# A larger planned margin on the q, k and v weight loads of a fused attention and feed-forward kernel

## The chip, the cores and the metric

The kernel runs on one core of one Trainium2 chip. The metric is the device time of one execution in microseconds, the median over runs. A core has TensorE (PE; its weight loads are PEld), VectorE (DVE), ScalarE (ACT), GpSimd (POOL) and SyncE (SP), which here issues all DMAs; the engines run side by side and meet at semaphores.

## What is computed

```python
def _A_ref(x, wqkv, wo):                      # x: 1 x 2048 x 576, 32 heads of 18
    qkv = (x @ wqkv) ...                      # q, k, v by heads
    scores = einsum("bhqd,bhkd->bhqk", q, k) * 18 ** -0.5
    mask = (i - j >= 0) & (i - j < 256)       # causal window of 256
    p = softmax(where(mask, scores, -1e9))
    return einsum("bhqk,bhkd->bhqd", p, v) ... @ wo

def _B_ref(x, w_gate, w_up, w_down):          # 576 -> 4608 -> 576
    return (sigmoid(x @ w_gate) * (x @ w_up)) @ w_down

xn = layernorm(x)
return x + _A_ref(xn) * silu(_B_ref(xn))
```

All inputs and the output are bf16; x has 2048 tokens of 576 features.

## The kernel before

The 2048 tokens are worked in four stages of 512 tokens, and each stage has four token blocks of 128. A stage normalises its blocks, brings them into `xn` (features on partitions, tokens along the free axis), projects q, k and v, and then runs two things interleaved on TensorE: the gate and up products of the feed-forward, 36 tiles of 128 hidden features, and the windowed attention, in eight head groups of four heads. The down projection (`f2`) closes the stage, and the next stage's projections stand inside it.

The matmuls have only 64 rows of contraction, so they go in pairs: one on the upper and one on the lower half of the array, side by side.

**A program that is planned, not written in order.** `Builder` makes a list of operations, each with an engine, an estimated length, the operations it depends on and a priority. `schedule` (L1083) simulates the five engines with these estimates and places the operations one by one: of those enabled on an engine it takes the one with the smallest start time plus `prio * PRIO_NS` (L1151 to L1164). The order in which operations are placed on an engine is the order in which that engine executes them. The estimates set only this order and the choice of PSUM banks; on the chip the waits are semaphores. For a DMA the planner computes when it should land, and its users are ready at

```python
                elif o.lane is not None:
                    t = o.done + o.slack
```

(L1210), so `slack` is a margin that the planner adds to one DMA's landing. It appears in no instruction.

**The first stage.** SyncE issues the four blocks of x, then twelve loads of `wqkv`: four parts each for q, then v, then k (`QKV_LOAD`), then the gate and up weights in groups of three tiles. `load9` splits a weight into four parts: parts 0 and 1 hold the first features for the lower and the upper half of the array, parts 2 and 3 the rest. `build_weights` sets the margin of the twelve loads:

```python
            for o in self.op_wqkv[j]:
                o.slack = QKV_SLACK
```

For the first stage TensorE transposes the normalised blocks (L487; two transposing steps a block, of 8 and of 10 matmuls), and ScalarE copies each result into `xn` (L499). `project` (L506, matmuls at L513) makes one projection of one block: 9 feature groups, two matmuls each, into one pair of PSUM banks, taken from (4, 5), (6, 7), (0, 1), (2, 3). For q of blocks 0 and 1 (`Q_SPLIT`) it is cut: a first part of 4 feature groups (8 matmuls), which needs only load parts 0 and 1 and the first of the two `xn` copies, and a second part of 5 (10 matmuls), which needs all four. ScalarE and VectorE then evict q and k (L567, into `pk` for block 0 and `expr` for the others) or v (L613, into `vau`). The places in `expr` are cleared by ScalarE first (L380), the third of these clearings after block 3's `xn` copies. When k of a block is evicted, a transposing DMA (L250) brings its q and k into `qkp`. VectorE spreads k from there (`kd`, L660), TensorE makes scores (L676, four steps a head group, units 0 to 3), ScalarE the exponential (L691), VectorE the mask (L705), TensorE the product with v (L733), VectorE the transposes and the division (L749 to L766).

The feed-forward steps (`f`, L884) use PSUM banks 4 to 7; the tanh on ScalarE (L898) and the multiply on VectorE (L902) free them. The scores use banks (0, 1) and (2, 3) in turn; the exponential frees them.

The order of TensorE at the start, before the change (`tr` are transposes; q0 is q of block 0; a and b are the first and second part):

```
warm-up, tr0, tr1, q0a, tr2, q0b, q1a, tr3, q1b, q2, v0, v1, v2, k0, v3, k1, q3, k2, k3, feed-forward
```

Of the kernel before, what the change touches and what calls it, by code (L numbers as in the profile page):

```python
# [100 lines left out]
QKT_BEHIND = {3: 0, 4: 1}  # L101
WARM = 10
X0_SLACK = -250.0
QKV_SLACK = 0.0
X_PRIO = (-9, -9, -9, -9)
QKV_LOAD = (-8, -6, -7)
W_PRIO = (-5, -4, -3, -2)
# [103 lines left out]
class Builder:  # L211
# [191 lines left out]
    def build_weights(self):  # L403
        wq = self.wqkv
        self.op_wqkv = [None] * 3
        for j in range(3):
# [3 lines left out]
            for o in self.op_wqkv[j]:  # L410
                o.slack = QKV_SLACK

# [932 lines left out]
```

## Time and profile before

| | |
|---|---|
| median of 3 runs | 561.78 us |
| lowest, highest | 561.67, 562.17 us |
| the profiled execution's own time | 561.61 us |
| its span | 559.9 us |
| TensorE busy | 552.2 us (99%) |
| VectorE, ScalarE, GpSimd busy | 317.7, 274.7, 30.0 us |
| DMA | 73.22 MB, mean 131 GB/s |

The profile is of one execution. Times are microseconds from the start of the span. "Releaser" is what ended an engine's wait; "idle" is rest of the engine just before an instruction. Matmuls overlap, and their ends are modelled, so the start to start distance tells more than the length of one.

### The profile page before, as it was taken

Reading aid. Unit: us, or ns where it says so; the run is one execution under the profiler, and the core shown is the slowest. Engines: PE = TensorE matmul, PEld = TensorE weight load, DVE = VectorE, ACT = ScalarE, POOL = GpSimd, SP = SyncE. Lnnn points to the kernel's source line nnn. Section 1 sums busy time; section 2 is a strip of 40 time slices with the busy share of each in tenths; the row PEclk is TensorE's granted clock in tenths of the full one; section 3 lists DMA queues with packets and bytes.
Section 4 is the critical chain, followed back from the end, with each engine's and each line's share of the span. In section 5 each row is a group of like instructions: output and inputs, shape, how many; then the busy total and the mean of one; then the engine's idle time right before and its main releaser. Section 6 shows DMA issues by size and latency. Waiting matters only on the chain.

```text
span 559.9 us, 16728 instructions
## 1 busy us (share of the span) xinstructions
PE 552.2 (99%) x7115; PEld 310.3 (55%) x7138; DVE 317.7 (57%) x911; ACT 274.7 (49%) x394; POOL 30.0 (5%) x58
## 2 busy tenths in 40 slices
PE   8999999999999999999999999999999999999997
PEld 5755555458555555455755555545665555554554
DVE  6436999334157989522417899841331788575012
ACT  8436876114076778221408776622131887482021
POOL 3000110100000100100000011010000000001000
PEclk9999999999999999999999999999999999999999
DMA  8999779859945665441993556543399354751010
GB/s 202 222 207 232 171 189 212 233 92 135 184 103 129 133 155 130 105 77 36 157 217 75 130 126 150 118 99 64 59 170 194 76 129 108 170 131 42 1 43 21
DMA packets 125921, 73.22 MB, mean 131 GB/s; under 512 B 54680, under 2 KB 125336, under 8 KB 125848
## 3 DMA queue, kind: packets, MB, share of 16 engines
q1 hardware_dynamic: 125848, 72.16, 61.3%
q8 instruction: 56, 0.92, 0.7%
q14 instruction: 17, 0.14, 0.1%
HBM read 55.48 MB, written 2.36 MB: 103 GB/s over the span
## 4 chain that ended last, share of the span: by engine, by line
PE 97%; DMA 1%; SPq 1%; issue 0%; ACT 0%; DVE 0%; ACTq 0%
PE ps L884 50%; PE ps L1009 23%; PE ps L513 9%; PE ps L676 6%; PE ps L733 4%; PE ps L802 3%; PE ps L1040 2%; DMA wqkv_sb<-in_A_wqkv_dram 1%; SPq L251 1%; DMA qkp<-pk 1%; ACT pk L567 0%; DVE expr L1073 0%; ACT expr L1071 0%; PE ps L487 0%; DVE expr L1075 0%
## 5 line engine op out<-in xcount | busy, mean ns | idle before, releaser
L884 PE MATMUL ps<-xn,wgs 64*128 64x512 bf16 x2522 | 299.7, 376 | 0.0
L884 PEld LDWEIGHTS ps<-xn,wgs 64*128 64x128 bf16 x2522 | 121.8, 94 | 113.6 <-issue 1.4
L691 ACT ACTIVATE expr<-ps 128x1024 bf16<-128x1024 f32 (+1 forms) x152 | 149.6, 1031 | 20.5 <-PE ps L676 20.5
L902 DVE SCALAR_TENSOR_TENSOR hT<-tring,ps 128x512 bf16<-128x512 bf16 x144 | 98.3, 683 | 63.3 <-PE ps L884 36.4
L1009 PE MATMUL ps<-wd_sb,hT 128*128 128x64 bf16 (+1 forms) x1057 | 131.1, 284 | 2.1 <-issue 1.1
L898 ACT ACTIVATE tring<-ps 128x512 bf16<-128x512 f32 x144 | 87.4, 607 | 91.8 <-PE ps L884 70.4
L1009 PEld LDWEIGHTS ps<-wd_sb,hT 128*128 128x128 bf16 x1080 | 68.2, 98 | 65.5 <-issue 2.5
L1071 ACT ACTIVATE expr<-ps 128x576 bf16<-128x576 f32 (+2 forms) x17 | 10.6, 623 | 127.8 <-PE ps L1009 120.2
L705 DVE TENSOR_TENSOR expr<-expr,m 128x256 bf16<-128x256 bf16 (+1 forms) x272 | 60.0, 265 | 4.3 <-ACT expr L691 4.1
L1073 DVE SCALAR_TENSOR_TENSOR expr<-expr,ps 128x576 bf16<-128x576 bf16 (+2 forms) x17 | 12.2, 719 | 84.1 <-ACT expr L1071 84.1
L676 PE MATMUL ps<-qkp,kd 64*128 64x320 bf16 (+4 forms) x720 | 57.1, 252 | 0.0
L513 PE MATMUL ps<-wqkv_sb,xn 64*128 64x288 bf16 x864 | 54.5, 283 | 0.5 <-DMA wqkv_sb<-in_A_wqkv_dram 0.4
L660 DVE TENSOR_SCALAR kd<-qkp,hm 128x256 bf16<-128x256 bf16 x176 | 40.5, 290 | 22.5 <-DMA qkp<-pk 20.8
L676 PEld LDWEIGHTS ps<-qkp,kd 64*128 64x128 bf16 x720 | 34.1, 94 | 34.1 <-issue 2.2
L513 PEld LDWEIGHTS ps<-wqkv_sb,xn 64*128 64x128 bf16 x864 | 44.4, 94 | 9.4 <-issue 1.4
L749 DVE STREAM_TRANSPOSE pk<-ps 128x512 f32<-128x512 f32 x32 | 21.5, 700 | 15.8 <-PE ps L733 15.8
L715 POOL COPY qkp<-qkp 128x256 bf16<-128x256 bf16 x24 | 10.8, 450 | 271.3 <-DVE kd L660 271.3
L766 DVE STREAM_TRANSPOSE op__63<-pk 128x512 bf16<-128x512 bf16 x32 | 22.2, 700 | 0.0
L733 PEld LDWEIGHTS ps<-expr,vau 64*32 64x32 bf16 x1440 | 18.1, 92 | 7.4 <-issue 4.7
L733 PE MATMUL ps<-expr,vau 64*32 64x320 bf16 (+4 forms) x1440 | 20.8, 254 | 0.0
L802 PE MATMUL ps<-wo_sb,oT 64*128 64x288 bf16 x288 | 18.7, 283 | 0.1
L613 DVE CAST vau<-ps 64x288 bf16<-64x288 f32 x32 | 14.6, 457 | 7.2 <-PE ps L513 6.6
(52 smaller groups left out, 192.5 us busy)
## 6 DMA issues: line engine op xcount, KB each, us to landing
wgs<-in_B_w_gate_dram SPq DMA_DIRECT2D x47, 240.0 KB, 3.8
wgs<-in_B_w_up_dram SPq DMA_DIRECT2D x47, 240.0 KB, 4.8
wgs<-in_B_w_up_dram SPq DMA_DIRECT2D x47, 192.0 KB, 4.0
wgs<-in_B_w_gate_dram SPq DMA_DIRECT2D x47, 192.0 KB, 4.6
wd_sb<-in_B_w_down_dram SPq DMA_DIRECT2D x9, 576.0 KB, 7.4
xf<-in_A_x_dram SPq DMA_DIRECT2D x18, 144.0 KB, 2.4
out_dram<-xf SPq DMA_DIRECT2D x15, 144.0 KB, 2.0
xr<-in_A_x_dram SPq DMA_DIRECT2D x14, 144.0 KB, 4.5
```

Source lines behind the costliest of these rows:

```text
L513: r = e.matmul(self.bank(ps, HV, hf), self.xn[r0:r0 + 64, k, i * P:(i + 1) * P], self.wqkv_sb[r0:r0 + 64, j, k, :], start=(k == 0), stop=( ...
L660: return e.tensor_scalar(dst, src, self.hm[:, half:half + 1], None, ALU.mult)
L676: i = e.matmul(self.bank(ps, 512, r)[:, pos * 64:(pos + n) * 64], w, self.qkp[r0:r0 + 64, hg, q0 * 64:(q0 + n) * 64], start=True, stop=Tru ...
L691: return e.activation(self.expr[:, es, :, 0:ncol], src, ACTF.Exp, scale=SM_SCALE)
L705: return e.tensor_tensor(ap, ap, m, ALU.mult)
L733: r = e.matmul(self.bank(ps2[s_])[32 * cg:32 * cg + 32, q0 * 64:(q0 + n) * 64], vf[:, v0:v0 + 32], self.expr[p0:p0 + 64, es, cg % 2, pos * ...
L766: t2 = self.op("DVE", dve_ns(CH), lambda e, on=on: e.transpose(self.op_[:, hg % NOT, :], on.rearrange("p g d -> p (g d)")), f"t2:{c}:{hg}" ...
L802: r = e.matmul(self.bank(ps2[w], HV, n), self.oT[r0:r0 + 64, kt, qi * P:(qi + 1) * P], self.wo_sb[r0:r0 + 64, kt, n * HV:(n + 1) * HV], st ...
L884: return e.matmul(self.bank((pg, pu)[gu][ft]), w, self.xn[r0:r0 + 64, i, :], start=first, stop=last, tile_position=(r0, 0))
L898: return e.activation(self.tring[:, st_, :], self.bank(ps), ACTF.Tanh, scale=0.5)
L902: return e.scalar_tensor_tensor(self.hT[:, ft, :], self.tring[:, st_, :], 1.0, self.bank(ps), ALU.add, ALU.mult)
L1009: r = e.matmul(self.ps[:, b + n0:b + n1], lhsT, self.wd_sb[:, q, fl, n0:n1], start=(ft == 0), stop=(ft == NFT - 1))
```

## The change

```diff
@@ -101,7 +101,7 @@
 QKT_BEHIND = {3: 0, 4: 1}
 WARM = 10
 X0_SLACK = -250.0
-QKV_SLACK = 0.0
+QKV_SLACK = 300.0
 X_PRIO = (-9, -9, -9, -9)
 QKV_LOAD = (-8, -6, -7)
 W_PRIO = (-5, -4, -3, -2)
```

The planner takes the twelve loads as landing 300 ns later. The plan that comes out has the same operations; SyncE and GpSimd keep their order. TensorE's order at the start becomes

```
warm-up, tr0, tr1, q0a, tr2, q1a, q0b, tr3, q1b, q2, q3, v0, v1, v2, k0, v3, k1, k2, k3, feed-forward
```

The banks of the later projections follow: q3 takes (6, 7), v0 (0, 1), v1 (2, 3), v2 (4, 5), k0 (6, 7), and so on, where v0 had (6, 7). ScalarE evicts q3 ahead of v0; VectorE does so too, and copies the lower half of the mask (L371) just ahead of the first eviction of q instead of behind it. Further on, around feed-forward tiles 17 to 25 of the first stage, the order shifts by a few places on three engines. On TensorE, the four score steps of head group 3 stand between other numbers of feed-forward matmuls:

```
before: f x10, sc3.0, f x8,  sc3.1, f x14, sc3.2, f x8,  sc3.3, f x10, sc4.0
after:  f x14, sc3.0, f x14, sc3.1, f x4,  sc3.2, f x14, sc3.3, f x4,  sc4.0
```

On ScalarE the tanh of tiles 20 and 21 change places with exponentials of group 3. On VectorE the transposes, divisions, masks and the multiplies of the tiles 17 to 24 are dealt differently among one another. From there on the order of every engine is as before, in this stage and the three others.

## Prediction

> **What bounds the kernel now.** I read the page first: its span, the busy shares, the clock and the chain.
>
> ```profile
> span 559.9 us, 16728 instructions
> PE 552.2 (99%) x7115; PEld 310.3 (55%) x7138; DVE 317.7 (57%) x911; ACT 274.7 (49%) x394; POOL 30.0 (5%) x58
> PEclk9999999999999999999999999999999999999999
> PE 97%; DMA 1%; SPq 1%; issue 0%; ACT 0%; DVE 0%; ACTq 0%
> ```
>
> TensorE works 552.2 of 559.9 us at full granted clock and carries 97% of the chain. A new order of the same matmuls can therefore give at most the 7.7 us in which it rests, and in the stage that is reordered only what it rests there. The view of waits, for TensorE over the whole run, has five rows:
>
> ```profile
> PE ps L388 <- DVE hm L373: 1.5, 1, 1.5
> PE ps L1009 <- issue: 1.1, 7, 0.2
> PE ps L513 <- DMA wqkv_sb<-in_A_wqkv_dram: 0.4, 1, 0.4
> PE ps L1009 <- ACT pk L567: 0.2, 1, 0.2
> PE ps L487 <- DVE xnr L461: 0.2, 1, 0.2
> ```
>
> One row belongs to the projections (L513): a single wait of 0.4 us for their weights. The timeline shows where it stands and what runs around it (start, length, engine, line, operation, count).
>
> ```profile
> 2.67 8.03 SPq L251 DMA_DIRECT2D wqkv_sb<-in_A_wqkv_dram  x12
> 7.04 0.67 PE L513 MATMUL ps<-wqkv_sb,xn 64*128 64x288 bf16 x8
> 8.75 1.28 PE L513 MATMUL ps<-wqkv_sb,xn 64*128 64x288 bf16 x18 [0.39 <-DMA wqkv_sb<-in_A_wqkv_dram]
> 9.64 0.46 DVE L567 CAST pk<-ps 128x288 bf16<-128x288 f32 x1 [0.43 <-PE ps L513]
> 9.85 0.44 PE L487 MATMUL ps<-op__63,xnr 64*128 64x64 bf16 x18
> 10.11 11.96 PE L513 MATMUL ps<-wqkv_sb,xn 64*128 64x288 bf16 x190
> 10.13 0.20 DVE L371 COPY m<-m 64x192 bf16<-64x192 bf16 x1
> 10.18 1.19 ACT L499 ACTIVATE xn<-ps 128x512 bf16<-128x512 bf16 x2
> 11.26 0.42 ACT L567 ACTIVATE expr<-ps 128x288 bf16<-128x288 f32 x1
> 11.55 1.07 ACT L380 ACTIVATE expr<-expr 128x1024 uint32<-128x1024 uint32 x1
> 15.25 0.27 PEld L513 LDWEIGHTS ps<-wqkv_sb,xn 64*128 64x128 bf16 x6 [0.24 <-issue]
> 21.89 17.66 PE L884 MATMUL ps<-xn,wgs 64*128 64x512 bf16 x162
> ```
>
> The 18 matmuls at 8.75 are the second q part of block 0 (10) and then the first q part of block 1 (8). They step in pairs: (9.85 - 8.75) / 9 = 0.122 us a pair, so a first part takes 0.49, a second part 0.61, a whole projection 1.10. The chain of waits names what the second part waits for:
>
> ```profile
> 4.79 3.82 DMA wqkv_sb<-in_A_wqkv_dram
> 8.61 0.14 issue
> ```
>
> The fourth q load, issued at 4.79, lands at 8.61, and TensorE starts 0.14 later. There is a second, smaller wait that the view of waits does not name. From 10.11 to 21.89 are 11.78 us for 190 matmuls; 95 pairs at 0.122 are 11.6, so 0.15 to 0.2 is lost, and the weight loads show one break, at 15.25. There the first k projection stands. The last of the 12 loads (the fourth k load) in the view of the tile, and its time to landing:
>
> ```profile
> L251 SPq DMA_DIRECT2D wqkv_sb<-in_A_wqkv_dram x1: 617/617/617, 10.1 to 10.1; - x1
> DMA to landing us min/median/max: 5.1/5.1/5.1
> ```
>
> It lands at about 15.2, just where the break is: k of block 0 waits for its weights too, about 0.15 us.
>
> **The change part by part.** Nothing is added or taken away: the same matmuls, evictions and DMAs, in the same order on SyncE and GpSimd. Three things move.
>
> First, the first q part of block 1 goes ahead of the second part of block 0. It needs only the first two q loads, which were there when block 0's first part began at 7.04, and the xn copies of block 1, which also free its bank:
>
> ```profile
> 7.50 0.72 ACT L499 ACTIVATE xn<-ps 128x640 bf16<-128x640 bf16 x1
> 8.64 0.70 ACT L499 ACTIVATE xn<-ps 128x640 bf16<-128x640 bf16 x1
> ```
>
> The first of these rows is that copy's second half: it ends at 8.22, and with 0.14 from release to start (the row of 8.61) the part begins at 8.36 and steps until 8.85. By then the load of 8.61 is there, so block 0's second part follows without a wait, 8.85 to 9.46. Block 3's transposes take 10.11 - 9.85 = 0.26; their bank is free when the second row ends at 9.34, plus 0.14 = 9.48 for their second half, which is in time. Block 1's second part starts at 9.72 instead of 10.11: 0.39 gained.
>
> Part of it is given back. q of block 2 writes the bank from which block 0's q is evicted. That eviction now follows a part that began at 8.85 and not 8.75, so it runs from 9.74 to 10.20 (0.46 us on VectorE), and block 2 starts at 10.34, against 9.72 + 0.61 = 10.33 without a wait: 0.01 lost. VectorE's mask copy (0.20, at L371), which now stands ahead of that eviction, fits into the 0.43 us of rest in the row of 9.64 and costs nothing.
>
> Second, q of block 3 comes straight after q of block 2, at 10.34 + 1.10 = 11.44, ahead of all v. It needs block 3's xn. ScalarE makes that after its half of block 0's eviction, which ends at 9.74 + 0.42 = 10.16 (the length of the row of 11.26); two copies take 1.19, so 11.35, plus 0.14 = 11.49. A new wait of 0.05. Taken together the projections now run 0.34 us ahead. The eviction of this q waits for ScalarE's clearing (1.07 us, at L380) and ends near 13.7; the projection that reuses its bank comes at 15.9, so that wait is covered by 2 us. If the clearing stood ahead of the xn copies, 1.07 us would be on the path; the planned order has it behind them.
>
> Third, what moves back: v by one projection and k of block 0 by one. v's loads had caused no wait and get 0.8 us more. k of block 0 starts at 15.28 - 0.34 + 1.10, near 16.0, when its load of 15.2 is there: the second wait, 0.15, goes as well.
>
> The sum: 0.34 + 0.15 = 0.49, say 0.5 us, and the feed-forward starts at 21.4 instead of 21.89. From both sides: the two waits whole give 0.39 + 0.15 = 0.54 and no more can come out of this stage; if the loads land where TensorE is anyway late, nothing is gained; below nothing it goes only by a new wait, which is a rival below.
>
> The planner's clock also moves a little, and near 63 us it deals the third group's score steps anew: between them stand 14, 14, 4, 14 and 4 feed-forward matmuls where 10, 8, 14, 8 and 10 stood. Work is equal; what can differ is the wait of a score step for the exponential that frees its bank.
>
> ```profile
> 64.03 0.38 PE L676 MATMUL ps<-qkp,kd 64*128 64x320 bf16 x4
> 65.33 1.68 PE L884 MATMUL ps<-xn,wgs 64*128 64x512 bf16 x14
> 66.84 0.38 PE L676 MATMUL ps<-qkp,kd 64*128 64x320 bf16 x4
> 69.17 0.38 PE L676 MATMUL ps<-qkp,kd 64*128 64x320 bf16 x4
> 64.30 0.60 ACT L898 ACTIVATE tring<-ps 128x512 bf16<-128x512 f32 x1 [0.33 <-PE ps L884]
> 64.79 1.93 ACT L691 ACTIVATE expr<-ps 128x1024 bf16<-128x1024 f32 x2
> ```
>
> On the old clock the three score steps now fall at 64.46, 66.19 and 66.84. ScalarE: exponential 64.96 to 65.98, tanh to 67.06 (0.6), second exponential to 68.0, third to 68.9 (1.02 each, overlapping by 0.1). The next group's first score step, at 69.17, needs the third: 68.9 + 0.14 = 69.06. It holds, with 0.1 us to spare. VectorE's transposes and masks around 62 to 72 us are dealt differently too, and are off the path while the matmuls' banks come free in time. I cost this move at nothing.
>
> Does the gain live to the end? What follows must not be bound by transfers on fixed times. SyncE issues the same list from 2.67 on and does not move. Rows of the views of tiles: the first group of gate and up weights, its last issue and its landings; the last two transposes of q and k, likewise; and the VectorE step that needs the last of them:
>
> ```profile
> L251 SPq DMA_DIRECT2D wgs<-in_B_w_up_dram x2: 626/1100/1575, 11.4 to 13.7; - x2
> DMA to landing us min/median/max: 5.0/5.5/5.8
> L250 SPq DMA_TRANSPOSE qkp<-expr x2: 2210/2372/2533, 37.5 to 39.8; - x2
> DMA to landing us min/median/max: 4.5/5.4/6.4
> 46.78 0.67 DVE L660 TENSOR_SCALAR kd<-qkp,hm 128x256 bf16<-128x256 bf16 x3
> ```
>
> The first group is there by 13.7 + 5.8 = 19.5 and is needed at 21.4. The last transpose, issued at 39.8, lands by 46.2; the VectorE step on it stands at 46.78 and comes to 46.3, so 0.1 us is left, and the scores behind it come 1 us later still. After that no transfer is named among TensorE's waits, in any stage, and those that SyncE issues behind a wait for TensorE move with it. So everything behind shifts together.
>
> **The sum against the times.** The profiled execution took 561.61 us (span 559.9 and 1.7 around it); the median of the three runs shown is 561.78, 0.17 more. Off the median the 0.5 gives 561.3. No change by a measurement of this kernel is about 0.2%, 1.1 us, so this gain, 0.09%, lies within it.
>
> A rule of the Trainium skill on the loads ("DMA: Bandwidth & Descriptors", Anatomy of one DMA) puts a transfer at about 2.0 us and its bytes at 436 GB/s, fitted on DMAs that GpSimd issues; for 180 KB that would be an estimated 2.4 us, all q weights would be there at 7.2, and the change would gain nothing. The trace disagrees: 3.8 us for that load and 5.1 for the last. What the traces leave of this rule is the second rival, at 0.10.
>
> **The rivals.**
>
> Given back in part (chance 0.14): the next release after the projections is late. For it, q of block 2 and q of block 3 start within 0.05 us of theirs, so 0.1 to 0.3 more on ScalarE goes straight onto the path. Against it, nothing later needs either. Time 561.5.
>
> No gain (0.10): the waits are an accident of the profiled execution, the loads land earlier otherwise, or a fixed transfer such as the transpose near 46 us takes the lead back. The view of the tile has, for all 12 of these loads:
>
> ```profile
> DMA to landing us min/median/max: 3.3/3.9/5.1
> ```
>
> With the quickest, 3.3 us, the fourth q load would be there at 8.1 and the part would wait 0.02. Against it, the profiled execution with both waits is quicker than the median. Time 561.8.
>
> The page's row of the multiply that frees a feed-forward bank:
>
> ```profile
> L902 DVE SCALAR_TENSOR_TENSOR hT<-tring,ps 128x512 bf16<-128x512 bf16 x144 | 98.3, 683 | 63.3 <-PE ps L884 36.4
> ```
>
> Slower (0.10): ScalarE becomes the bound near 69 us. If the third exponential ends after 69.03, the next score step waits, the tanh behind it is late, the VectorE multiply behind that too, and the feed-forward finds no bank: 1.02 + 0.60 + 0.69 = 2.3 us, less 0.5, so 563.6. For it, the margin of 0.1; against it, a late release costs only its own lateness, usually, because 14 matmuls (1.5 us) follow.
>
> Faster by more than 0.2% (0.06): the loads land later without the profiler and both waits are longer. It needs 1.1 us; 560.5.
>
> **How the numbers follow.** The forecast, 561.3, has 0.60. Forecast, part and no gain together, 0.84, lie between 561.2 and 561.8; runs of one kernel differ by 0.5 (561.67 to 562.17), so the range is 560.9 to 562.2. Chances: faster 0.06, same 0.84, slower 0.10.
>
> **What would show it.** Right: no wait on the q weights, or one below 0.1; block 1's first part at 8.4 and its second near 9.7; no break at the first k projection; the feed-forward at 21.4; the span 0.5 shorter, and no rest of TensorE near 64 to 69. Wrong: a wait for ScalarE at L513 above 0.1, a wait at L676 or L884 near 69, or a feed-forward that starts at 21.4 and a second stage that starts as late as before.

## The result and the profile after

| | before | after |
|---|---|---|
| median (22 runs each, side by side) | 561.98 us | 561.23 us |
| lowest, highest | 561.29, 562.82 | 560.85, 561.64 |
| ratio, 95% interval | | 0.9987 [0.9981, 0.9992] |
| the profiled execution | 561.61 us, span 559.9 | 560.9 us, span 559.2 |
| feed-forward starts | 21.89 us | 21.37 us |
| final projection (L1040) starts | 547.80 us | 547.06 us |

The change gains 0.75 us by the medians (0.4 to 1.1 by the interval), 0.73 us by the two profiles. Both lie within the 0.2% that was called no change beforehand. A later series of the changed kernel gives 561.24 beside a median of 561.88 for the kernel before: 0.64. Two executions of the later runs (580.26 us of the kernel before and 580.66 of the last variant below) were slow at a granted clock of 0.95 and are left out of the medians here. Forecast were 561.3 us and a gain of 0.5.

TensorE at the start, in the timeline of the kernel after (start, length, engine, line, operation, count; in brackets the rest before it and what ended it), with the rows of ScalarE that mattered:

```profile
6.88 0.67 PE L513 MATMUL ps<-wqkv_sb,xn 64*128 64x288 bf16 x8
7.86 0.54 PE L487 MATMUL ps<-op__63,xnr 64*128 64x64 bf16 x18 [0.32 <-DVE mv L454]
8.35 1.28 PE L513 MATMUL ps<-wqkv_sb,xn 64*128 64x288 bf16 x18
9.46 0.43 PE L487 MATMUL ps<-op__63,xnr 64*128 64x64 bf16 x18
9.72 11.82 PE L513 MATMUL ps<-wqkv_sb,xn 64*128 64x288 bf16 x190
21.37 2.34 PE L884 MATMUL ps<-xn,wgs 64*128 64x512 bf16 x20
9.73 0.41 ACT L567 ACTIVATE pk<-ps 128x288 bf16<-128x288 f32 x1 [0.35 <-PE ps L513]
10.04 1.19 ACT L499 ACTIVATE xn<-ps 128x512 bf16<-128x512 bf16 x2
```

The 18 matmuls that stood at 8.75 behind a wait of 0.39 now stand at 8.35 with none: the first part of block 1 (8 matmuls), and behind it the second part of block 0 (10). The last 190 begin at 9.72 instead of 10.11, and the start of the feed-forward is 11.65 us behind them, not 11.78: 95 pairs at 0.122 without a break. The stage is 0.52 us shorter.

The view of waits for TensorE, whole run, has two rows in the kernel after:

```profile
PE ps L388 <- DVE hm L373: 1.5, 1, 1.5
PE ps L487 <- DVE mv L454: 0.3, 1, 0.3
```

The row for the weights is gone, but so are the L1009 rows of 1.1 and 0.2 us, which this change cannot have touched. A second profile of the very same kernel has them back. From its page and its view of waits, and behind them the row of the page of the first profile:

```profile
L1009 PE MATMUL ps<-wd_sb,hT 128*128 128x64 bf16 (+1 forms) x1057 | 131.1, 285 | 2.1 <-issue 1.1
PE ps L1009 <- issue: 1.1, 7, 0.2
PE ps L1009 <- ACT pk L567: 0.2, 1, 0.2
```

```profile
L1009 PE MATMUL ps<-wd_sb,hT 128*128 128x512 bf16 (+1 forms) x1080 | 133.7, 287 | 0.0
```

The kernel has 1080 of these matmuls; in a trace with 1057 records, 23 are missing, and their place reads as rest. The profile of before also has 1057, so 1.3 of the waits in it were none.

### The profile page after: what moved, and what is told of

It is laid out like the page before. It is cut to its first block, busy times and chain, and to the rows that moved or that the text cites. A ratio compares the mean times of both kernels' runs of the same rounds, so it can differ in the third digit from the quotient of the medians.

```text
span 559.2 us, 16752 instructions
## 1 busy us (share of the span) xinstructions
PE 553.9 (99%) x7138; PEld 308.5 (55%) x7138; DVE 317.8 (57%) x911; ACT 274.5 (49%) x394; POOL 29.4 (5%) x58
## 4 chain that ended last, share of the span: by engine, by line
PE 98%; DVE 1%; DMA 0%; issue 0%; ACT 0%
PE ps L884 50%; PE ps L1009 24%; PE ps L513 9%; PE ps L676 6%; PE ps L733 4%; PE ps L802 3%; PE ps L1040 2%; DMA xr<-in_A_x_dram 0%; DVE bnst L452 0%; DVE bnst L450 0%; DVE xnr L461 0%; PE ps L487 0%; DVE mv L454 0%; DVE expr L1073 0%; ACT expr L1071 0%
## 5 line engine op out<-in xcount | busy, mean ns | idle before, releaser
L1009 PE MATMUL ps<-wd_sb,hT 128*128 128x512 bf16 (+1 forms) x1080 | 133.7, 287 | 0.0
L1009 PEld LDWEIGHTS ps<-wd_sb,hT 128*128 128x128 bf16 x1080 | 68.1, 98 | 65.6 <-issue 2.2
L749 DVE STREAM_TRANSPOSE pk<-ps 128x512 f32<-128x512 f32 x32 | 21.6, 701 | 15.9 <-PE ps L733 15.9
```

The source lines that it names most:

```text
L1009: r = e.matmul(self.ps[:, b + n0:b + n1], lhsT, self.wd_sb[:, q, fl, n0:n1], start=(ft == 0), stop=(ft == NFT - 1))
```

## Experiments

The theory that went on record (A): the gain is the removal of two waits in the first stage, that of block 0's second q part for the fourth q load and that of block 0's k for the last k load; they are coupled, since the k load lands when it lands. Rival B: each move adds its own part. Rival C: part of the gain does not come from the projections but from the new deal of the third head group's score steps. Theory D came up in the study and is told at its place.

The 95% intervals of the runs below are about 0.5 us to either side, so most of these medians can't be told apart; the argument rests on the starts and waits in the profiles.

**One move alone.** `QKV_SLACK` split by q, v, k. First only q's margin: block 1's first part goes ahead of block 0's second, q of block 3 stays, and the new deal comes along.

```diff
-QKV_SLACK = 0.0
+QKV_SLACK = (300.0, 0.0, 0.0)
-                o.slack = QKV_SLACK
+                o.slack = QKV_SLACK[j]
```

> Only the first move: block 1's first q part ahead of block 0's second, with the new deal of the score steps; q of block 3 stays behind k of block 1. Theory A (the two waits are coupled by the landing of the last k load, a fixed time near 15.0 to 15.2): the first wait goes, but k of block 0 comes free 0.38 us earlier, near 14.75, and must still wait for its load, so that wait grows from 0.15 to 0.3 to 0.5; feed-forward starts near 21.7 to 21.9, gain over before 0 to 0.2 us. Rival B (the two moves add up): feed-forward near 21.5, gain 0.35 to 0.4, k's wait stays 0.15. Rival C (the new deal of the score steps brings part of the gain): beyond the feed-forward's start, 0.1 to 0.3 us more is gained between 60 and 110 us.

Measured: 561.74 us, ratio 0.9996 [0.9987, 1.0005]; feed-forward at 21.69. Then only k's margin, which brings q of block 3 ahead of v, with the deal as before (the expectation calls the first run e1):

```diff
+QKV_SLACK = (0.0, 0.0, 300.0)
```

> Only the second move: q of block 3 ahead of all v; block 0's second q part stays ahead of block 1's first, and the score steps keep the deal of before. Theory A: the wait of 0.4 for the fourth q load stays, the one at k goes; feed-forward near 21.75, gain 0.15. With e1 this adds up to 0.15 to 0.35 and not to the 0.52 that both moves give together. Rival B: likewise 0.15 here, and the sum with e1 is 0.5. Rival C: nothing gained beyond the feed-forward's start.

Measured: 561.71 us, 0.9993 [0.9984, 1.0002]; feed-forward at 21.93. Two rows of the first one's timeline, then two of the second one's:

```profile
8.68 1.28 PE L513 MATMUL ps<-wqkv_sb,xn 64*128 64x288 bf16 x18 [0.28 <-ACT xn L499]
10.05 11.82 PE L513 MATMUL ps<-wqkv_sb,xn 64*128 64x288 bf16 x190
```

```profile
8.93 1.28 PE L513 MATMUL ps<-wqkv_sb,xn 64*128 64x288 bf16 x18 [0.54 <-DMA wqkv_sb<-in_A_wqkv_dram]
10.29 11.82 PE L513 MATMUL ps<-wqkv_sb,xn 64*128 64x288 bf16 x190
```

Each takes away the wait that it should: the first has no wait on a load, the second has its k without a break (21.93 - 10.29 = 11.64). But the loads did not stand still: the fourth q load, at 8.61 in the profile of before, landed at 8.51 and 8.80, the last k load, at 15.14, at 14.14 and 15.34, and block 1's `xn` was 0.3 later in the first. Neither run tells A from B: with the k load at 14.14 nothing couples. In the first, block 1's second part starts at 10.05, only 0.06 ahead of 10.11: this move alone did not bring its 0.39 there.

**The deal alone, and the projections alone.** The planner's estimate of one operation, v of block 3, is changed by 102.6 ns; that moves no instruction of the projections, but the later deal. The changed projections with the old deal:

```diff
-        o = self.pe((NC - k0) * mm_ns(HV), ...
+        o = self.pe((NC - k0) * mm_ns(HV) + (-102.6 if name == 'v:3' else 0.0), ...
```

> The changed kernel with the score steps, tanh and VectorE work from the feed-forward on dealt as before; the projections as in the changed kernel. Theory A: feed-forward at 21.4, and the same time as the changed kernel within 0.1 us, about 0.5 below before. Rival C (the deal brings 0.1 to 0.3): 0.1 to 0.3 us slower than the changed kernel, its lead over before shrinks behind 60 us.

Measured: 561.67 us, 0.9992 [0.9984, 1.0001]; feed-forward at 21.69. The old projections with the new deal (the same line in the kernel before, with +102.6):

> The kernel before with the score steps dealt as in the changed kernel; the projections as before, both waits kept. Theory A: feed-forward at 21.9, the same time as before within 0.1 us. Rival C: 0.1 to 0.3 us faster than before, gained between 60 and 110 us.

Measured: 561.71 us, 0.9993 [0.9985, 1.0002]. Its first stage is the slowest of all, because the last k load landed at 15.93:

```profile
9.99 5.35 PE L513 MATMUL ps<-wqkv_sb,xn 64*128 64x288 bf16 x82
16.07 6.79 PE L513 MATMUL ps<-wqkv_sb,xn 64*128 64x288 bf16 x108 [0.73 <-DMA wqkv_sb<-in_A_wqkv_dram]
22.68 0.61 PE L884 MATMUL ps<-xn,wgs 64*128 64x512 bf16 x4
```

This is the break of 15.25 grown to 0.73 us of rest, 0.89 by the distance of the starts (1.01 instead of 0.12): A's second wait, in the order of before. And yet this kernel's median is no worse than that of the other. Behind the first stage it was quicker: from the start of the feed-forward to that of the final projection it took 525.74 us, the changed kernel 525.70, the kernel before 525.91 and the one with the old deal 526.22. C has something to explain, then: about 0.2 us that the prediction had at nothing, and more in the run with the old deal, which has a wait of its own (below).

**The landing made late.** To test A without waiting for chance, one load of 295 KB is issued between the v loads and the k loads, in the kernel before and in the changed kernel; it brings half of a group of down weights that is loaded again later.

```diff
+        self.extra = self.dma(self.wd_sb[:, NWD - 1, 0:2, :], ..., prio=-6.5, issue=0.0)
...
+        self.op_wd[-1].add_dep(self.extra)
```

In the kernel before:

> The kernel before, with one extra load of 295 KB issued between the v loads and the k loads (the first half of the last group of down weights; its regular load comes again later), so that the k loads land later; the planned order is unchanged. Theory A (the stage's second wait hangs on the landing of the last k load, and only the kernel before is exposed to it): the last k load lands near 16, 0.9 to 1.0 us later than in the profiles so far, k of block 0 waits for all of that, the feed-forward starts near 22.8 instead of 21.9 and the time is 0.8 to 1.0 us above the kernel before, about 562.9. Rival (the landing of k is no term; the gain is all in the q parts): the feed-forward starts at 21.9 and the time is that of the kernel before.

In the changed kernel:

> The changed kernel with the same extra load of 295 KB ahead of the k loads. Theory A: k of block 0 stands near 15.9 here, so a landing near 16 costs only 0.1 to 0.3; feed-forward near 21.6, time 0.1 to 0.3 above the changed kernel, and 1.2 to 1.5 below the same edit of the kernel before. Rival: both kernels take the edit alike, and the difference between the two stays at 0.5 to 0.75.

Measured: 563.44 us (1.0029 [1.0018, 1.0039]) and 562.03 us (1.0002 [0.9994, 1.0011]), 1.41 apart. The timelines, of the first and of the second:

```profile
16.73 6.79 PE L517 MATMUL ps<-wqkv_sb,xn 64*128 64x288 bf16 x108 [1.26 <-DMA wqkv_sb<-in_A_wqkv_dram]
23.34 0.40 PE L888 MATMUL ps<-xn,wgs 64*128 64x512 bf16 x2
```

```profile
16.44 5.69 PE L517 MATMUL ps<-wqkv_sb,xn 64*128 64x288 bf16 x90 [0.46 <-DMA wqkv_sb<-in_A_wqkv_dram]
21.95 1.91 PE L888 MATMUL ps<-xn,wgs 64*128 64x512 bf16 x16
```

The k loads moved further than expected, to 16.6 and 16.3, so that the changed kernel also waits, 0.46, and takes 0.8 more than without the extra load, not 0.1 to 0.3. But the difference grew from 0.75 to 1.41 us, as A says and its rival does not. The intervals of the two ratios alone would leave that open; the rows show it, with a rest of 1.26 against 0.46. In the profile of before, what the k load is later than 15.0 is lost, in that of the changed kernel only what it is later than 15.7 (its k of block 0 starts at 15.85). One term of the gain is therefore no fixed number but depends on an execution's landing.

**The same two kernels again.**

> The changed kernel unchanged, for a second profiled execution. Theory A (the landings move from one execution to the next, and this kernel is late enough to hide them): the last k load lands anywhere from 14.1 to 15.9, TensorE shows no wait at the first k projection, the feed-forward starts at 21.35 to 21.40; ratio to the kernel before 0.9985 to 0.9992. Theory C (bank parity of the score steps): no wait ahead of the score step near 163 us.

> The kernel before unchanged, for a second profiled execution. Theory A: the wait of the second q part follows the landing of the fourth q load (8.3 to 8.8) and the wait at the first k projection that of the last k load (none up to 15.0, 0.9 at 15.9), so the feed-forward starts anywhere from 21.7 to 22.7. Theory C: the score step near 163 us waits 0.11 again, because its banks are the other pair. Ratio 1.0000 within its interval, which gives the noise of a comparison.

Measured: 561.24 us (0.9988 [0.9979, 0.9997]) and 562.09 us (1.0005 [0.9996, 1.0014]). From the second profile of the kernel before, the timeline and the view of the weight tile (the last three of the loads, and their time to landing):

```profile
15.76 6.79 PE L513 MATMUL ps<-wqkv_sb,xn 64*128 64x288 bf16 x108 [0.57 <-DVE vau L613]
22.37 1.47 PE L884 MATMUL ps<-xn,wgs 64*128 64x512 bf16 x12
L251 SPq DMA_DIRECT2D wqkv_sb<-in_A_wqkv_dram x3: 616/617/622, 8.8 to 10.1; - x3
DMA to landing us min/median/max: 4.0/5.4/5.5
```

The wait at k is 0.57 here. The row blames an eviction of v, but the last load, issued at 10.1, landed 5.5 us later, at 15.6, and TensorE started 0.14 after that, as in the profile of before. In the second profile of the changed kernel the load landed at 15.3, there is no break, and the feed-forward starts at 21.25.

All profiles with the loads as they are and with both moves or neither, by the order of the projections:

| projections | profile | transposes begin | last 190 begin | last k load lands | feed-forward starts |
|---|---|---|---|---|---|
| old | before | 5.62 | 10.11 | 15.14 | 21.89 |
| old | before again | 5.90 | 9.99 | 15.62 | 22.37 |
| old | old projections, new deal | 5.90 | 9.99 | 15.93 | 22.68 |
| old | index moved (below) | 5.90 | 9.95 | 14.79 | 21.59 |
| new | after | 5.68 | 9.72 | 14.95 | 21.37 |
| new | after again | 5.58 | 9.61 | 15.30 | 21.25 |
| new | old deal | 5.90 | 10.05 | 14.22 | 21.69 |
| new | old deal, index moved (below) | 5.91 | 10.05 | 15.82 | 21.69 |

The mean is 22.13 for the old order and 21.50 for the new: 0.63 us, with 21.59 to 22.68 on the one side and 21.25 to 21.69 on the other. In these four the new order's start does not depend on k; what is left of its spread comes from block 1's `xn`, 0.3 us later in the last two.

The two moves do not share the 0.63 as the first pair of profiles has it. Up to the start of the last 190 matmuls, which is where the first move tells, the means are 10.01 and 9.86: 0.15. From there to the feed-forward they are 12.12 and 11.64: 0.48, nearly all of it the wait for k. The column of the transposes says why. `xn` follows them, and they follow ten warm-up matmuls, whose pace differs between executions. The timelines of the kernel before, first and second profile:

```profile
1.52 3.94 PE L388 MATMUL ps<-hT 128*128 128x512 bf16 x10 [1.52 <-DVE hm L373]
```

```profile
1.52 4.45 PE L388 MATMUL ps<-hT 128*128 128x512 bf16 x10 [1.52 <-DVE hm L373]
```

In the second all ten start 0.43 us apart, in the first the last two only 0.38 and 0.21 behind the one ahead. So block 1's `xn` is there at 8.22 in the first and at 8.62 in the second. Of the twelve profiles read, four are of the first kind (before, after, after again, and the changed kernel with the late load: 3.71 to 4.23 us for the ten, transposes from 5.58 to 5.68), eight of the second (4.45, transposes from 5.90). In the second kind the new order waits for `xn` and starts the last 190 at 10.05, the old one at 9.95 to 9.99 when the fourth q load lands at 8.28 to 8.47, and at 10.29 when it lands at 8.80 (k's margin alone): the first move then gains only if that load is late, and else loses 0.06 to 0.10. Why the pace differs no run shows; the granted clock reads 1.00 in both. Nor do so few profiles show how often each kind comes, so 0.15 and 0.48 are means of these four and four, no more.

**Where the deal gains.** Ahead of the score step at 163.58, the kernel before takes 1.19 us for 10 feed-forward matmuls (162.39 to 163.58), the kernel after 1.08 (161.92 to 163.00). VectorE around it in the kernel before:

```profile
161.44 0.29 DVE L705 TENSOR_TENSOR expr<-expr,m 128x256 bf16<-128x256 bf16 x1
162.35 0.69 DVE L902 SCALAR_TENSOR_TENSOR hT<-tring,ps 128x512 bf16<-128x512 bf16 x1 [0.62 <-PE ps L884]
162.39 1.24 PE L884 MATMUL ps<-xn,wgs 64*128 64x512 bf16 x10
163.58 0.39 PE L676 MATMUL ps<-qkp,kd 64*128 64x320 bf16 x4
```

and in the kernel after:

```profile
160.96 0.29 DVE L705 TENSOR_TENSOR expr<-expr,m 128x256 bf16<-128x256 bf16 x1
161.52 0.69 DVE L902 SCALAR_TENSOR_TENSOR hT<-tring,ps 128x512 bf16<-128x512 bf16 x1 [0.27 <-PE ps L884]
161.92 1.24 PE L884 MATMUL ps<-xn,wgs 64*128 64x512 bf16 x10
163.00 0.38 PE L676 MATMUL ps<-qkp,kd 64*128 64x320 bf16 x4
```

The multiply waits for the same two semaphores at the same counts in both. In the kernel after it starts 0.09 us behind the later one, in the kernel before 0.45, although the releasing matmul ended at 161.91. Two things differ: from the new deal on, the score steps have the other of their two bank pairs, and VectorE's list has one wait instruction more, so that this multiply, which was number 320 of that list (counted from 1 in the trace, waits included), is number 321. In the kernel before, number 576 starts late too, and 576 - 320 = 256. The timelines of before, and then of after, where this addition is number 577:

```profile
266.32 0.46 DVE L1077 TENSOR_TENSOR xf<-xf,expr 128x576 bf16<-128x576 bf16 x1 [0.46 <-DVE expr L1075]
```

```profile
265.38 0.46 DVE L1077 TENSOR_TENSOR xf<-xf,expr 128x576 bf16<-128x576 bf16 x1
```

It rests 0.46 behind the instruction just ahead of it on its own engine; in the kernel after that distance is 0.10. The load that it also needs had landed at 238.48. Theory D: the number costs, not the banks. Test: the kernel before with one VectorE instruction more at its start, all else the same.

```diff
-self.op_negh = op("DVE", 60, lambda e: e.memset(self.neghalf[:, :], -0.5), ...
+self.op_negh = op("DVE", 60, lambda e: (e.memset(self.neghalf[0:64, :], -0.5), e.memset(self.neghalf[64:P, :], -0.5))[1], ...
```

> The kernel before with one VectorE instruction more at its start (a memset of 128x1 cut into two of 64x1), order, banks and deal unchanged. In both profiles of the kernel before the multiply at 162.36 (162.87 in the second), which is the instruction of index 320 of VectorE's list, starts 0.447 us after the later of its semaphores and the end of the instruction ahead of it, and the feed-forward group of 10 matmuls there takes 1.19 us; in the changed kernel the same multiply has index 321, starts 0.088 us after, and the group takes 1.08. Theory D (the index in the list costs, not the order or the banks): here the multiply has index 321, starts 0.09 after and the group takes 1.08; time 0.1 below the kernel before. Rival (the other pair of score banks): 0.447 and 1.19 as before, same time.

The timeline, at the same place and at an earlier one:

```profile
162.02 0.69 DVE L902 SCALAR_TENSOR_TENSOR hT<-tring,ps 128x512 bf16<-128x512 bf16 x1 [0.27 <-PE ps L884]
162.42 1.24 PE L884 MATMUL ps<-xn,wgs 64*128 64x512 bf16 x10
163.50 0.38 PE L676 MATMUL ps<-qkp,kd 64*128 64x320 bf16 x4
30.33 0.69 DVE L902 SCALAR_TENSOR_TENSOR hT<-tring,ps 128x512 bf16<-128x512 bf16 x1 [1.26 <-ACT tring L898]
32.70 0.69 DVE L902 SCALAR_TENSOR_TENSOR hT<-tring,ps 128x512 bf16<-128x512 bf16 x1 [1.68 <-PE ps L884]
34.22 0.69 DVE L902 SCALAR_TENSOR_TENSOR hT<-tring,ps 128x512 bf16<-128x512 bf16 x1 [0.83 <-ACT tring L898]
```

The wait at 162 is gone, 1.08 us for the group, with the banks of before: D, not the banks. The time did not fall (561.94 us, ratio 1.0000 [0.9992, 1.0009]), which D had not foreseen: the step of one brought another multiply onto number 64 (320 - 256), the one at 32.70, which starts 0.43 us later than its neighbours' rhythm of 1.94 (30.33, 34.22) has it. That one was dearer: TensorE has lost 0.29 us by the next score step, at 48. All twelve profiles agree: where this multiply and this addition are numbers 320 and 576 (five profiles, all with the old deal), both start about 0.45 behind their last release; where they are 321 and 577 (seven, of both deals), neither does.

> The changed projections with the old deal of score steps, and one VectorE instruction more at the start. Theory D: the multiply near 162 starts 0.09 after its releases and the group takes 1.08; from the start of the feed-forward to the start of the final projection 525.73 to 525.80 us, as with the new deal, if the transposes land in time; time as the changed kernel, 561.2 to 561.4. Rival (banks of the new deal): the wait of 0.11 stays, 525.9 or more, time 561.6 to 561.7 as with the old deal alone.

Measured: 561.46 us, 0.9991 [0.9982, 1.0000]. Again 1.08 for the group at 162, again the late multiply (32.81), and 525.95 us from the feed-forward to the final projection instead of 525.73 to 525.80: 0.15 to 0.22 too many, for the same reason (0.29 is lost by the score step at 48). The median lies between the two forecasts; the group's 1.08 us is what speaks for D. In the kernel after, the numbers 64, 320 and 576 all fall on wait instructions, and no late start shows.

What is left of C are two places where the kernel before at times waits for a transposing DMA. The rows are from the timelines of the run with the old deal, and then of the kernel before:

```profile
295.46 0.48 DVE L660 TENSOR_SCALAR kd<-qkp,hm 128x256 bf16<-128x256 bf16 x2 [7.51 <-DMA qkp<-pk]
296.75 0.40 PE L676 MATMUL ps<-qkp,kd 64*128 64x320 bf16 x6 [0.24 <-DVE expr L1073]
```

```profile
293.80 0.48 DVE L660 TENSOR_SCALAR kd<-qkp,hm 128x256 bf16<-128x256 bf16 x2 [5.64 <-DMA qkp<-pk]
296.55 0.38 PE L676 MATMUL ps<-qkp,kd 64*128 64x320 bf16 x6
```

The transpose landed 9.8 us after its issue in the one and 7.5 in the other, and the score step lost 0.40. In the second profile of before it lost 0.32 there; in the first profile of before, 0.10 at the like place of the fourth stage (434). None of the five profiles with the new deal that were read shows it, three of the seven with the old deal do. This transpose took 7.3 to 7.6 us in the five and 7.4 to 9.8 in the seven. Whether the deal has a part in that or chance has, these runs do not settle. From the feed-forward to the final projection the remaining profiles took 525.81 (k's margin alone) and 526.17 (before again) with the old deal, 525.73 twice (q's margin alone, after again) with the new, 526.03 with the list moved by one, and with the late load 525.80 before and 525.95 after; what the last of these lost, 0.07 ahead of 48 and 0.16 between 89 and 157, has not been explained.

**More cover.** The changed kernel with v of block 3 ahead of k of block 0 as well:

```diff
-QKV_SLACK = 300.0
+QKV_SLACK = (300.0, 2000.0, 300.0)
```

> The changed kernel with v's margin at 2000, so that v of block 3 also goes ahead of k of block 0, which then starts near 17.0 instead of 15.9. Theory A: the last k load lands at 14.1 to 16.6 in the executions so far, so the changed kernel is still late in some; here none is. In a profile with a landing before 15.9 the feed-forward starts at 21.25 to 21.4 as in the changed kernel; the median falls by 0 to 0.2 us. Rival (the landing of k is no term any more): the same time within 0.1.

Measured: 561.24 us, 0.9987 [0.9978, 0.9996]; only the time is read. It equals the changed kernel's 561.24, which both forecasts allow. In the four profiles of the new order with the loads as they are k of block 0 never waited, so there was nothing left to cover. Nothing tried here is better than the changed kernel.

## Why the prediction was right, and where it was not

The time came out at 561.23 where 561.3 was forecast, inside the range and, as the likeliest case had it, within 0.2% of no change. The mechanism, two waits for loads that a new order covers, is what the runs show. That the sum came so close is in part luck: taken over several profiles its two terms are off in opposite directions. Step by step:

- *Block 1's first part at 8.36, its second at 9.72*: 8.35 and 9.72. Right for this pair of profiles, 0.39 gained. Over four profiles each it is 0.15: in two of the new ones block 1's `xn` comes 0.3 later, and in three of the old ones the fourth q load lands ahead of 8.61.
- *New waits of 0.01 at q of block 2 and 0.05 at q of block 3*: neither showed. ScalarE's `xn` copies began at 10.04, not 10.16: they overlap the eviction that ends at 10.14. So they end at 11.23, and block 3's q had its data at 11.37, ahead of 11.44. The price was 0.06 too high.
- *No break at the first k projection*: right, and the lever is larger than 0.15. That was one execution's landing; the old order loses 0 to 0.89 there by the distance of the starts (landings of 14.79 to 15.93), 0.48 in the mean of the stage's second part. So both terms are mis-sized, 0.15 for 0.39 and 0.48 for 0.15, and the stage gains 0.63, not 0.49. The bound that no more than 0.54 can come out of the stage was one execution's too. That the runs of before are the wider ones (1.5 us against 0.8 for the kernel after) fits with the wait for k.
- *Feed-forward at 21.4*: 21.37 and 21.25, but 21.69 where `xn` of block 1 came late. That this start can move was not in the prediction.
- *The new deal costs nothing near 64 to 69 us*: right at its place. TensorE there in the kernel after:

```profile
66.32 0.38 PE L676 MATMUL ps<-qkp,kd 64*128 64x320 bf16 x4
66.54 1.68 PE L884 MATMUL ps<-xn,wgs 64*128 64x512 bf16 x14
68.05 0.33 PE L676 MATMUL ps<-qkp,kd 64*128 64x256 bf16 x4
68.64 0.38 PE L676 MATMUL ps<-qkp,kd 64*128 64x320 bf16 x4
66.43 1.94 ACT L691 ACTIVATE expr<-ps 128x1024 bf16<-128x1024 f32 x2
```

  14 matmuls take 1.51 us, as elsewhere; the third exponential ends at 68.37, and the next group's score step, at 68.64 instead of 69.17, keeps the lead of 0.53. The rival of the slower side, a bound on ScalarE, did not come.
- *The deal counted at nothing, everything behind shifts together*: the step that failed. The lead is 0.52 at the feed-forward and 0.73 at the final projection. Of the rest, 0.11 comes at 162 from the number of an instruction in VectorE's list, and 0.10 at 434, where the score step waits for a transpose in the profile of before; smaller gains and losses, 0.05 at most, cancel. The order of the instructions had been compared, not their number. "After that no transfer is named" was true of one execution only.
- *TensorE rests 7.7 us in all*: some of this was missing records (1057 of 1080), so the bound was looser than it looked. Nothing hung on it.

- *The rival of loads that land early, so that nothing is gained*: the fourth q load landed between 8.28 and 8.80 in all profiles with the loads unchanged. In the old order block 0's second part stood at 8.42 to 8.93, always 0.14 behind it. Even so part of the rival holds: where `xn` was late and this load was not, the old order begins its last 190 matmuls no later than the new one, and only the wait for k is gained.

The sizes therefore add up as 0.5 to 0.6 in the first stage and 0.1 to 0.2 behind it; 0.64 to 0.75 by the medians (0.85 against the second series of the kernel before).

## What to carry to other kernels

A wait for a load that one profile shows at 0.15 us is one draw: profile the same kernel twice, or make the load late on purpose, before pricing it, and count an order that keeps work ahead of the load as a gain in spread too. Compare the terms one by one over all profiles, and not only the sum. Before an "issue" wait on TensorE is believed, compare the count of its matmuls with what the program has. When a change touches one stage and time comes or goes in another, look at the number of instructions on each engine, not only at their order.

## What the runs showed of the hardware

An instruction of VectorE at number 64, 320 or 576 of its list (steps of 256) started 0.35 to 0.43 us late where it was due at once: 0.45 instead of 0.09 at 162.35 and 0.45 instead of 0.10 at 266.32 in the kernel before, 0.53 instead of 0.10 at 32.70 with the list moved by one. Numbers 832 and 1088 showed nothing, nor did a number that fell on a wait instruction. Why the steps of 256 begin at 64 no run shows. The page of the kernel after has a queue that fetches instructions:

```profile
q8 instruction: 56, 0.92, 0.7%
```

0.92 MB in 56 packets are 16.4 KB each. The Trainium skill ("Runtime: NRT & Kernel Launch", Instruction fetch mechanics) says that an engine's instructions are refilled in blocks of 16 KiB, 256 instructions, and that crossing a block is mostly hidden. Packet size and the step of 256 agree with it; the price of 0.35 to 0.43 at three of five crossings, 0.11 and 0.29 of it on the path, goes beyond "mostly hidden". That the fetch is the cause is inferred from this agreement; no run shows the fetch itself.

The other surprise is the spread of landings between executions of the same instructions: 14.1 to 15.9 us for the last k load over the profiles with the loads unchanged, 7.3 to 9.8 us from issue to landing for one transposing DMA. The pace of TensorE's ten warm-up matmuls differs between executions too, 3.71 to 4.45 us for the ten, while the granted clock reads 1.00.
